# Two multiplications move from VectorE to GpSimd, one more pack of scores moves to VectorE, in a new order

## The chip, the core and the metric

The kernel runs on one core of one Trainium2 chip. The metric is the time of one execution on the device, in microseconds (us). The core's engines work side by side, each through its own queue in order: TensorE (PE in the profile, PEld for its weight loads), VectorE (DVE), ScalarE (ACT), GpSimd (POOL) and SyncE (SP, which issues the transfers). They wait for one another by semaphores. SBUF is the on-chip memory, PSUM the eight banks into which TensorE writes.

## What is computed

Two attention branches over the same x (2048 tokens, width 512, 32 heads of 16), mixed by a gate per token:

```python
def _A_ref(x, wqkv, wo):
    ...
    scores = jnp.einsum("bhqd,bhkd->bhqk", q, k) * (Dh ** -0.5)
    p = _softmax(scores, axis=-1)
    o = jnp.einsum("bhqk,bhkd->bhqd", p, v)
    ...
def _B_ref(x, wqkv, w_phi, wo):
    ...
    pq = jnp.einsum("bhsd,hdf->bhsf", q, w_phi)
    pk = jnp.einsum("bhsd,hdf->bhsf", k, w_phi)
    phi_q = jnp.concatenate([_softmax(pq, axis=-1), _softmax(-pq, axis=-1)], axis=-1)
    phi_k = jnp.concatenate([_softmax(pk, axis=-1), _softmax(-pk, axis=-1)], axis=-1)
    kv = jnp.einsum("bhsf,bhsd->bhfd", phi_k, v)
    z  = jnp.einsum("bhsf->bhf", phi_k)
    num = jnp.einsum("bhqf,bhfd->bhqd", phi_q, kv)
    den = jnp.einsum("bhqf,bhf->bhq", phi_q, z)[..., None] + 1e-6
    o = num / den
    ...
x = A_x
g = _sigmoid((x * gate_w).sum(-1, keepdims=True))
a = _A_ref(x, A_wqkv, A_wo)
b = _B_ref(x, B_wqkv, B_w_phi, B_wo)
return g * a + (1 - g) * b
```

Branch A is full attention: 32 heads x 2048 queries x 2048 keys of exponentials. Branch B is linear attention with "hedgehog" maps (the softmax of a projection and of its negative, over 16 features).

## The kernel before

**Packs and groups.** A unit is a tile of 128 keys by 512 queries of one head. A pack is four units: the same tile for four heads, whose matmuls run in four row or column quarters of TensorE. There are 512 packs: 4 chunks of queries, 8 sets of four heads, 16 tiles of keys; 32 groups `g` of 16 packs each (one chunk and one set of heads). Within a group the values are summed in one PSUM bank.

**Two ways to the exponential.** For most packs ScalarE computes it: `_qk` writes scores into a ring of five PSUM banks (`RING`), three and two units in turn, `_exp` (L1183) turns a group of them into ET in one instruction of 1536 or 1024 columns, `_pv` multiplies by the values. `self.mine` is the list of ScalarE's units; a unit's bank is its place in that list modulo 5. The scores of group k wait for the exponentials of group k - 2. The first five units and the last pack are done in two halves of 256 queries. `_last_pack` cuts the last four units in two pieces where the ring wraps inside them, and asks for all scores of a piece in one instruction, after the exponentials of the units that held its banks before (ScalarE's own lines there are L1070).

For the packs that `AWAY` names VectorE approximates: `_vector_bits` (L962, `v_bits`) converts each unit's scores to the bits of a power of two, and `_vector_terms` makes two more terms with shifted bits, by VectorE (L984, `v_term`, for a pair of packs in one instruction of 4096 elements, or 2048 for a single pack) and by GpSimd (L999, `p_term`, two instructions of 1024 per pack). Each such pack needs three rounds of value matmuls (L1250) where ScalarE's need one. `AWAY` has one number per group; each of its bits 0 to 4 names a tile of keys, and pack 510 is added at the end. Its 32 numbers have 130 bits set, in 76 pairs of which 22 are single.

**The end of a group.** `_norm` transposes the bank into T1 (L1271, `n_t1`), and for each two groups GpSimd multiplies the denominators with the gate (L1278, `n_den`), VectorE takes the reciprocal (L1280, `n_rec`) and multiplies the values with it into T2 (L1282, `n_mul`). Transfers turn T2 into onTA, which the output matmuls read (L651). Group 30 does this alone, group 31 in `_norm_last` in two halves (L1105 to L1117).

**Branch B.** `_b_quad` does four tiles of tokens at once: projections into bq (L1395), trees for maximum and minimum (L1414), subtraction (L1423), the exponentials on ScalarE (L1425), sums (L1430, L1432, and L1434 on GpSimd), and `_b_scale`, which gives reciprocals and multiplies half of bq with them: `b_rec`, `b_ratio` (on GpSimd), `b_mul` (L1450 for keys, L1455 for queries, VectorE, 2048 elements each). There are four quads for keys and four for queries. The maps then go to the key-value matmuls (L1473) or, by transposing transfers, to the numerator's (L1533).

**The order.** Nothing is ordered by hand in the instruction lists. Each operation is given to `Plan.op` with an engine, a cost in us, a due time in packs (`prio`) and an earliest time (`rel`), and `Plan.order` walks through time and picks for each engine what is ready and due first; the lists that it makes are the engines' programs. `SHIFT` moves the due times of named pieces (`b106`, `p102`, `x13`, ...) by up to 14 packs. Operations of GpSimd, and those of VectorE whose names are in `PORT` (`v_term`, `b_max`, `b_sub`, `b_sum`, `b_mul`, `n_mul` and others), are kept apart in the plan's time, and a GpSimd operation waits by semaphore for the last such operation of VectorE that the plan put ahead of it:

```python
if o.port:
    t = max(t, port, held.end + held.lat if held is not None and e == "POOL" else 0.0)
```

TensorE fills gaps with matmuls on zeros (L1257, `_fill`).

Of the kernel before, what the change touches and what calls it, by code (L numbers as in the profile page):

```python
# [7 lines left out]
ALU = mybir.AluOpType  # L8
AX = mybir.AxisListType

P = 128
# [378 lines left out]
class _Kernel:  # L390
# [364 lines left out]
    def _gate(self):  # L755
# [44 lines left out]
    AWAY = (26, 27, 26, 31, 22, 13, 15, 15, 31, 15, 13, 31, 30, 23, 31, 15, 29, 31, 26, 27, 31, 26, 31, 21, 31, 31, 28, 31, 31, 11, 23, 31)  # L800

    SHIFT = (
# [463 lines left out]
    def _norm(self, qc, src, side, last, dst, b_dst, due, job, alone=False):  # L1266

        op = self.plan.op
        T1, T2, rinv = self.T1, self.T2, self.rinv
# [6 lines left out]
        n, reads = hi - lo, b_T1[lo:hi]  # L1276
# [393 lines left out]
```

## Time and profile before

| | us |
|---|---|
| median of 3 runs | 737.42 (737.13 to 737.89) |
| profiled execution, whole | 737.4 |
| its span, first to last instruction | 735.6 |
| ScalarE busy | 723.5 |
| TensorE busy | 713.1 |
| VectorE busy | 690.5 |
| GpSimd busy | 303.8 |

The profile is one execution. A group's row has the line, the engine, the operation, what it writes and reads with its size, the count, the busy time in us, the mean of one in ns, and the idle time before it with what ended it. A timeline row has the start in us from the span's start, the length of a stretch of equal instructions and what they are; rows of one engine can overlap, since an instruction's record goes on while the next one starts. A wait's row names who waited for whom, the total in us, how many times, and the longest.

### The profile page before, as it was taken

How to read it: one execution, taken by the hardware profiler on the slowest of the kernel's cores; microseconds unless marked ns; L12 is line 12 of the kernel's file. 1: busy time of each engine (PE TensorE's matmuls, PEld its weight loads, DVE VectorE, ACT ScalarE, POOL GpSimd, SP SyncE). 2: the span in 40 equal slices, each digit the busy share in tenths (PEclk: the TensorE clock that was granted, in tenths of full speed). 3: DMA queues.
4: the chain of work that ended last, by engine and by line, in shares of the span. 5: the costliest groups of instructions: out<-in, count | busy, mean ns of one | idle time of the engine just before them, and what ended most of it. 6: DMA issues, size and time to landing. Idle time of an engine off the chain costs nothing.

```text
span 735.6 us, 19777 instructions
## 1 busy us (share of the span) xinstructions
PE 713.1 (97%) x8549; PEld 234.4 (32%) x8549; DVE 690.5 (94%) x1085; ACT 723.5 (98%) x636; POOL 303.8 (41%) x318
## 2 busy tenths in 40 slices
PE   8999999999999999999999999999999999999998
PEld 3334233243223223332232233333332233332322
DVE  4899999988999999999999999999999999999996
ACT  6999999999999999999999999999999999999996
POOL 3832342424544424535353344334334444344442
PEclk9999999999999999999999999999999999999999
DMA  9400100001010010100001032042123111003210
GB/s 201 145 10 6 22 2 9 16 4 18 4 15 11 4 20 2 17 11 8 14 2 17 15 61 28 8 83 35 23 45 74 21 16 23 16 25 63 40 29 30
DMA packets 90041, 21.96 MB, mean 30 GB/s; under 512 B 82913, under 2 KB 89441, under 8 KB 89953
## 3 DMA queue, kind: packets, MB, share of 16 engines
q1 hardware_dynamic: 88752, 20.30, 14.5%
q8 instruction: 67, 1.10, 0.7%
q10 hardware_dynamic: 1200, 0.39, 0.2%
q14 instruction: 22, 0.17, 0.1%
HBM read 4.21 MB, written 2.10 MB: 9 GB/s over the span
## 4 chain that ended last, share of the span: by engine, by line
ACT 73%; PE 13%; DVE 11%; DMA 1%; issue 0%; POOL 0%; DVEq 0%; POOLq 0%
ACT ET L1183 70%; PE ps L1131 5%; DVE va L962 4%; PE ps L1250 4%; ACT bq L1425 3%; PE ps L651 2%; DVE vp L984 2%; DVE btree L1414 1%; DMA xT<-in_A_x_dram 1%; PE ps L744 1%; PE ps L1257 1%; DVE bq L1423 0%; DVE VB L1541 0%; DVE nb L1541 0%; DVE rb L1539 0%
## 5 line engine op out<-in xcount | busy, mean ns | idle before, releaser
L1183 ACT ACTIVATE ET<-ps 128x1536 bf16<-128x1536 f32 (+1 forms) x612 | 692.9, 1343 | 4.6 <-PE ps L1131 4.4
L999 POOL TENSOR_SCALAR vp<-va 128x1024 uint16<-128x1024 uint16 x264 | 275.7, 1044 | 337.3 <-DVE vp L984 124.2
L962 DVE TENSOR_SCALAR va<-ps 128x512 uint16<-128x512 f32 x520 | 339.5, 681 | 23.9 <-PE ps L1131 21.7
L1131 PE MATMUL ps<-qT,kT 32*128 32x512 bf16 (+1 forms) x2053 | 311.0, 384 | 10.1 <-ACT ET L1183 5.1
L1131 PEld LDWEIGHTS ps<-qT,kT 32*128 32x128 bf16 x2053 | 82.7, 91 | 258.3 <-ACT ET L1183 146.5
L984 DVE TENSOR_SCALAR vp<-va 128x4096 uint16<-128x4096 uint16 (+1 forms) x151 | 162.0, 1079 | 0.6 <-PE ps L1250 0.2
L1250 PE MATMUL ps<-ET,V 128*32 128x512 bf16 x1532 | 149.0, 385 | 1.3 <-DVE T L1271 1.0
L1250 PE MATMUL ps<-vp,vc 128*32 128x512 bf16 x1040 | 93.9, 384 | 0.3 <-DVE vp L984 0.2
L1250 PEld LDWEIGHTS ps<-ET,V 128*32 128x32 bf16 x1532 | 39.3, 95 | 64.9 <-issue 48.6
L651 PE MATMUL ps<-WB,xT 128*32 128x512 bf16 x768 | 57.4, 382 | 0.5 <-DVE bq L1395 0.3
L1250 PE MATMUL ps<-va,V 128*32 128x512 bf16 x520 | 51.3, 385 | 0.0
L1250 PE MATMUL ps<-vp,V 128*32 128x512 bf16 x520 | 48.2, 383 | 0.3 <-DVE vp L984 0.2
L1257 PE MATMUL ps<-kT,zero 128*32 128x512 bf16 x468 | 42.1, 384 | 0.0
L651 PE MATMUL ps<-xT,WA 128*32 128x512 bf16 x480 | 36.1, 382 | 0.6 <-DVE va L962 0.4
L1250 PEld LDWEIGHTS ps<-vp,vc 128*32 128x32 bf16 x1040 | 24.7, 95 | 35.3 <-issue 20.2
L1425 ACT ACTIVATE bq<-bq 128x2048 bf16<-128x2048 bf16 x16 | 31.5, 1989 | 0.1
L1271 DVE STREAM_TRANSPOSE T<-ps 128x512 f32<-128x512 f32 x31 | 21.9, 708 | 1.1 <-PE ps L1250 1.0
L651 PE MATMUL ps<-WoB,WT 128*32 128x512 bf16 x256 | 22.6, 383 | 0.3 <-DVE va L962 0.3
L1395 DVE CAST bq<-ps 128x512 bf16<-128x512 f32 x32 | 21.7, 678 | 0.3 <-PE ps L651 0.2
L651 PEld LDWEIGHTS ps<-WB,xT 128*32 128x32 bf16 x768 | 15.2, 95 | 19.9 <-issue 10.4
L651 PE MATMUL ps<-WoA,onTA 128*32 128x512 bf16 x256 | 21.2, 381 | 0.0
L744 PE MATMUL ps<-WA,xT 128*128 128x128 bf16 x256 | 19.5, 220 | 0.7 <-DVE va L962 0.4
(94 smaller groups left out, 367.1 us busy)
## 6 DMA issues: line engine op xcount, KB each, us to landing
turned<-T SPq DMA_DIRECT2D x240, 8.0 KB, 1.8
qT<-qs SPq DMA_DIRECT2D x120, 16.0 KB, 1.8
WB<-in_B_wqkv_dram SPq DMA_DIRECT2D x1, 1536.0 KB, 6.9
out_dram<-WB SPq DMA_DIRECT2D x12, 128.0 KB, 2.0
WA<-in_A_wqkv_dram SPq DMA_DIRECT2D x3, 384.0 KB, 5.1
WoA<-in_A_wo_dram SPq DMA_DIRECT2D x1, 512.0 KB, 8.0
WoB<-in_B_wo_dram SPq DMA_DIRECT2D x1, 512.0 KB, 8.9
out_dram<-xT SPq DMA_DIRECT2D x3, 128.0 KB, 1.8
```

Source lines behind the costliest of these rows:

```text
L651: ins = e.matmul(out[32 * g:32 * g + 32], lhs[:, 32 * g:32 * g + 32], rhs, start=start, stop=stop, tile_position=(0, 32 * g), skip_group_c ...
L744: ins = e.matmul(self._bank(job)[:, P * tt:P * tt + P], self.xT[:, c, QCH * j + TOK * tt:QCH * j + TOK * tt + TOK], self.WA[:, 2, c, P * c ...
L962: parts.append(op("DVE", lambda e, j=j, job=job: e.tensor_scalar(self.va[:, pair, side, j, :], self._bank(job), SCALE * LOG2E * 128.0, (12 ...
L984: self.plan.op("DVE", lambda e, k=k, shift=shift: e.tensor_scalar(flat(self.vp[:, k]), flat(self.va[:, pair]), float(shift), None, op0=ALU ...
L999: o = self.plan.op("POOL", lambda e, flat=flat: e.tensor_scalar(flat[0], flat[1], 1.0, float(shift), op0=ALU.mult, op1=ALU.add), 0.08 + n ...
L1131: return e.matmul(out, self.kT[32 * i:32 * i + 32, cp, kt * TOK:(kt + 1) * TOK], self.qT[32 * i:32 * i + 32, s, at], start=True, stop=True ...
L1183: o = plan.op("ACT", lambda e: e.activation(self.ET[:, a % NS:a % NS + n, at], self.ps[:, self._ring(a):self._ring(a) + n, at], ACT.Exp, s ...
L1250: ins = e.matmul(self._bank(ot)[32 * i:32 * i + 32, at], V[:, v0:v0 + 32], tile(), start=(kt == 0), stop=(kt == self.NT - 1), tile_positio ...
L1257: ins = e.matmul(self._bank(ot)[32 * i:32 * i + 32, :], self.zero[:], self.kT[:, 0, 0:QCH], start=False, stop=False, tile_position=(0, 32 ...
L1271: self.turned_out = op("DVE", lambda e: e.transpose(T1[:, side].rearrange("p b s -> p (b s)"), src()), 0.635, deps=last, writes=[b_T1[side ...
L1395: [lambda e, b, k=k: e.tensor_copy(bq[:, k].rearrange("p (g s v) -> p g s v", g=8, s=2)[:, :, 0, :], b.rearrange("p (g v) -> p g v", g=8))],
L1425: op("ACT", lambda e, side=side: e.activation(sides[side], sides[side], ACT.Exp, scale=1.0 - 2 * side), self.c_act(2048) + 0.04, reads=[bu ...
```

## The change

1. `n_mul` is given to GpSimd, and its cost in the plan goes from 0.065 + 0.269 n to 0.31 + 0.3 n (n is 2 for a pair of groups, 1 for group 30).
2. `b_mul` is given to GpSimd, in two pieces of 1024 elements, each at a cost of 1.52.
3. `AWAY` has other numbers: 131 bits set, in 76 pairs of which 21 are single. `SHIFT` has other entries throughout.

```diff
-    AWAY = (26, 27, 26, 31, 22, 13, 15, 15, 31, 15, 13, 31, 30, 23, 31, 15, 29, 31, 26, 27, 31, 26, 31, 21, 31, 31, 28, 31, 31, 11, 23, 31)
+    AWAY = (22, 27, 13, 23, 11, 28, 26, 31, 31, 31, 14, 31, 31, 15, 29, 23, 15, 31, 22, 31, 27, 22, 31, 15, 30, 31, 30, 31, 30, 31, 11, 31)
...
-        op("DVE", lambda e: e.tensor_tensor(
+        op("POOL", lambda e: e.tensor_tensor(
             T2[:].rearrange("p b (s d) -> p s b d", s=2)[:, lo:hi], T1[:, lo:hi, :, 0:16],
-            rinv[:, lo:hi, :, None].to_broadcast([P, n, 16, 16]), ALU.mult), 0.065 + 0.269 * n,
+            rinv[:, lo:hi, :, None].to_broadcast([P, n, 16, 16]), ALU.mult), 0.31 + 0.3 * n,
            reads=reads + [b_rinv], writes=[b_T2], name="n_mul", prio=due)
...
         def run(name, cost, fn, at, reads, writes):
-            eng = "POOL" if name in ("b_ratio", "b_tot") else "DVE"
+            eng = "POOL" if name in ("b_ratio", "b_tot", "b_mul") else "DVE"
...
-                    ("b_mul", two(2048), lambda e: e.tensor_tensor(x[:, 0::2], x[:, 0::2], spread(r, 32), ALU.mult),
-                     b_r + both, [both[0]])]
+                    *[("b_mul", 1.52, lambda e, a=a: e.tensor_tensor(
+                        x[:, a:a + 32:2], x[:, a:a + 32:2], spread(r[:, a // 2:a // 2 + 16], 16), ALU.mult),
+                       b_r + both, [both[0]]) for a in (0, 32)]]
...
-                ("b_mul", two(2048), lambda e: e.tensor_tensor(x[:, 1::2], x[:, 1::2], spread(r, 32), ALU.mult),
-                 b_r + both, [both[1]])]
+                *[("b_mul", 1.52, lambda e, a=a: e.tensor_tensor(
+                    x[:, a + 1:a + 32:2], x[:, a + 1:a + 32:2], spread(r[:, a // 2:a // 2 + 16], 16), ALU.mult),
+                   b_r + both, [both[1]]) for a in (0, 32)]]
```

206 rows, old and new, of the table SHIFT are left out of this document.

## The prediction

> **What bounds the kernel now.** I read the page's busy times first, then the groups of ScalarE's instructions by shape, then what ScalarE waited for, then the chain that ended last.
>
> ```profile
> span 735.6 us, 19777 instructions
> PE 713.1 (97%) x8549; PEld 234.4 (32%) x8549; DVE 690.5 (94%) x1085; ACT 723.5 (98%) x636; POOL 303.8 (41%) x318
> ...
> ACT ET L1183 <- PE ps L1131: 4.4, 1, 4.4
> ACT xT L1619 <- PE ps L651: 2.9, 1, 2.9
> ...
> L1183 ACT ACTIVATE ET<-ps 128x1536 bf16<-128x1536 f32 x304 | 473.7, 1558 | 0.2
> L1183 ACT ACTIVATE ET<-ps 128x1024 bf16<-128x1024 f32 x303 | 344.8, 1138 | 0.0
> L1183 ACT ACTIVATE ET<-ps 128x512 bf16<-128x512 f32 x3 | 1.8, 601 | 0.0
> ...
> 550.71 94.97 ACT ET L1183 x84
> ...
> L1257 PE MATMUL ps<-kT,zero 128*32 128x512 bf16 x468 | 42.1, 384 | 0.0
> ```
>
> Three engines are over 90% busy, but only ScalarE (ACT) has no idle time between its start and its tail: it waits 4.4 us for the first scores and 2.9 us for the last output, and nowhere else by this view. PE's 97% holds filler work (468 matmuls of L1257), and VectorE has gaps. So a unit of exponentials (512 columns) taken from ScalarE shortens the run, if PE and VectorE go on feeding it. The records overlap at their ends, so the price of a group is the distance of two starts:
>
> ```profile
> 723.95 2.36 ACT L1183 ACTIVATE ET<-ps 128x1024 bf16<-128x1024 f32 x2
> 724.86 1.46 ACT L1183 ACTIVATE ET<-ps 128x1536 bf16<-128x1536 f32 x1
> ...
> 726.19 0.62 ACT L1183 ACTIVATE ET<-ps 128x512 bf16<-128x512 f32 x1
> 726.66 1.12 ACT L1070 ACTIVATE ET<-ps 128x256 bf16<-128x256 f32 x2
> 726.93 0.86 ACT L1070 ACTIVATE ET<-ps 128x768 bf16<-128x768 f32 x1
> ```
>
> A group of 1024 columns costs 0.91 us (723.95 to 724.86), one of 1536 1.33, one of 512 0.47: 2.24 for a pair of three and two units. The chain's stretch of 84 groups is 42 pairs of 2.26. The 0.02 between is small waiting that the records' overlap hides; over 303 pairs it is about 6 us, and it can shrink or grow.
>
> **The change part by part.** AWAY has 130 bits set before and 131 after: one more pack of four units goes to VectorE. ScalarE has 1528 units before: 5 in halves, 303 pairs of groups, then 3 + 1 left over, then the last pack's 4. After, 1524: 5, exactly 303 pairs, no leftover, and the last 4. The leftover groups go: 1.33 + 0.47 = 1.80 us less.
>
> The same arithmetic moves the end. Units sit in a ring of five banks. Before, the last pack starts in the fifth bank, so its scores go in two pieces, one unit and three, and the piece of three needs only banks that were freed one group earlier. After, it starts at unit 1520, bank 0, in one piece of four, and needs the banks of the last two groups, so it cannot start before the very last normal group is done.
>
> ```profile
> 7.09 0.28 PE L1131 MATMUL ps<-qT,kT 32*128 32x256 bf16 x3 [0.23 <-DVE qT L724]
> ...
> 7.42 9.61 ACT L1183 ACTIVATE ET<-ps 128x768 bf16<-128x768 f32 x10 [4.38 <-PE ps L1131]
> ...
> 726.37 0.39 PE L1131 MATMUL ps<-qT,kT 32*128 32x512 bf16 x3 [0.22 <-ACT ET L1183]
> ```
>
> PE starts 0.05 us after a group's record ends (724.86 + 1.46 = 726.32, then 726.37). From scores to exponential it is 0.33 us where nothing else holds it (7.09 to 7.42, 256 columns); full columns add 0.11 (0.39 against 0.28): 0.44. So the last group's start is followed not 0.91 but 1.14 + 0.05 + 0.44 = 1.63 us later by the last pack: 0.72 us of new idle time. The first half of the last pack then takes 1.14 as one group, as before (726.66 to 727.79). Net so far: -1.80 + 0.72 = -1.08 us.
>
> ```profile
> 726.92 1.04 POOL L999 TENSOR_SCALAR vp<-va 128x1024 uint16<-128x1024 uint16 x1 [1.85 <-DVE vp L984]
> ...
> 728.00 0.28 PE L1250 MATMUL ps<-ET,V 128*32 128x256 bf16 x4
> 728.02 0.10 PEld L1250 LDWEIGHTS ps<-vp,vc 128*32 128x32 bf16 x4
> ...
> 728.55 0.45 DVE L1105 STREAM_TRANSPOSE T<-ps 128x256 f32<-128x256 f32 x1 [1.72 <-PE ps L1250]
> ```
>
> The tail's first transpose also waits for the last term of pack 510, which GpSimd ends at 727.96: it starts at 728.55, while the values alone end at 728.28. Up to 0.27 us comes back if VectorE runs less late there; I take half, -0.15.
>
> VectorE loses eight b_mul and sixteen n_mul (g 0 to 29 in fifteen pairs, g 30 alone):
>
> ```profile
> L1282 DVE TENSOR_TENSOR T<-T,rinv 128x512 bf16<-128x512 f32 x15 | 10.4, 691 | 0.0
> L1455 DVE TENSOR_TENSOR bq<-bq,brec 128x2048 bf16<-128x2048 bf16 x4 | 4.8, 1212 | 0.0
> L1450 DVE TENSOR_TENSOR bq<-bq,brec 128x2048 bf16<-128x2048 bf16 x4 | 4.8, 1211 | 0.0
> ...
> 32.19 1.19 DVE va L962 x2
> ...
> L984 DVE TENSOR_SCALAR vp<-va 128x4096 uint16<-128x4096 uint16 x107 | 132.0, 1237 | 0.6 <-PE ps L1250 0.2
> L984 DVE TENSOR_SCALAR vp<-va 128x2048 uint16<-128x2048 uint16 x44 | 30.3, 695 | 0.1
> ```
>
> That is 20 us of records. It gains four bit conversions of 0.60 (two in 1.19) and, since one single pack becomes a pair, two additions that grow from 0.70 to 1.24: 3.5. VectorE falls by some 16 us, 2%. GpSimd gains them in other prices, which no row shows at these sizes:
>
> ```profile
> L999 POOL TENSOR_SCALAR vp<-va 128x1024 uint16<-128x1024 uint16 x264 | 275.7, 1044 | 337.3 <-DVE vp L984 124.2 <-DVE va L962 90.5 <-PE ps L1250 69.7
> L1434 POOL TENSOR_TENSOR bsum<-btree 128x256 f32<-128x256 f16 x8 | 4.9, 612 | 31.3 <-DVE vp L984 15.1 <-DVE btree L1432 11.1 <-DVE T L1282 5.0
> L1454 POOL TENSOR_TENSOR brec<-bsum 128x128 f16<-128x128 f32 x4 | 1.8, 456 | 1.8 <-DVE bsum L1453 1.6
> ...
> L1278 POOL TENSOR_TENSOR rinv<-T,gh x16: 258/264/1306, 64.8 to 712.9; 128x32 f32<-128x32 f32 x15, 128x16 f32<-128x16 f32 x1
> ...
>   PEld ps L1250: 2.2, 8
> ```
>
> Bounds for one b_mul piece of 1024 elements: 1.04 us (the one-input row of that size) and 2.45 (four times the two-input row of 256). From the two two-input rows the slope is 156 ns per 128 elements: 612 + 6 x 156 = 1.55 us, which I take, since they are the same kind of instruction; n_mul by the same slope 0.92, within 0.52 and 1.22. (From the 32-element row's median, 264, the slope is steeper: 1.55 ns per element, 1.80 us for a piece.) GpSimd gains 16 x 1.55 + 15.5 x 0.92 + two more terms of 1.04 = 41 us, to 345 of 734: never the bound by its sum.
>
> GpSimd's queue is in order: behind a multiply that waits for VectorE's reciprocal stand the terms of L999, for which PE's value matmuls wait. The last row is from the list of those who waited for L999: PE's weight loads, 2.2 us in all, so terms usually come early; the cover is that lead. The hedgehog maps come some 2 us later (two pieces of 1.55 for 1.21) to the transposes and to the key-value matmuls, which are due 2 steps of 3.45 packs, near 10 us, after the multiply. No cover, no such lead: each late term would stop PE for its delay. The extra pack costs PE two more rounds of four value matmuls, hidden in filler.
>
> The price that matters is what VectorE's two-input and 16-bit instructions and GpSimd's do to each other:
>
> ```profile
> 712.84 1.22 DVE L984 TENSOR_SCALAR vp<-va 128x4096 uint16<-128x4096 uint16 x1
> 712.89 1.25 POOL L1278 TENSOR_TENSOR rinv<-T,gh 128x16 f32<-128x16 f32 x1
> ...
> 720.96 1.04 POOL L999 TENSOR_SCALAR vp<-va 128x1024 uint16<-128x1024 uint16 x1 [1.16 <-DVE vp L984]
> ...
> 721.39 1.69 DVE L984 TENSOR_SCALAR vp<-va 128x4096 uint16<-128x4096 uint16 x1
> ```
>
> A product of 16 elements took 1.25 us because VectorE's addition was under way; an addition took 1.69 instead of 1.22 because GpSimd's term was. One holds the other off for its whole length. The order written out keeps them apart by its own costs (b_mul 1.52, n_mul 0.91), and the mean of 1237 against 1.22 shows that it mostly succeeds. With 1.55 and 0.92 it would still.
>
> [...]
>
> VectorE, freed of 16 us, holds PE up less. PE's own waits:
>
> ```profile
> PEld ps L1131 <- ACT ET L1183: 146.5, 365, 1.1
> ...
> PEld ps L1131 <- DVE va L962: 33.6, 98, 0.7
> ```
>
> Of ScalarE's 6 us of small waiting I let 0.5 go: an estimate, 2% less VectorE work and a new order that can as well be worse; bounds +1.5 and -3.
>
> Sum against the profiled execution's own 737.4 (span 735.6 and 1.8 around it; the median of the runs is 737.42): 737.4 - 1.08 - 0.15 - 0.5 = **735.7 us**.
>
> **The rivals.** (1) Slower: GpSimd's multiplies are longer than the order allows. At the upper bound of 2.45 us a piece holds the lock 0.93 us past its 1.52, and VectorE's next addition, tree step or subtraction stops for that; its conversions come late, PE stops in order behind their banks, ScalarE's next scores behind that. PE's lead over ScalarE is about 0.40 us (146.5 over 365 waits), so it decides from an overrun of 0.4 us, a piece of 1.9; n_mul's bound, 0.31 past its 0.91, stays below that. A hit costs 0.53; 16 of them 8.5 us, and with half falling where VectorE has conversions to do instead 4.2: 735.7 + 4.2 = 739.9. For it: the steeper slope, 1.80 a piece. Against: VectorE still has some 60 us idle to catch up in.
>
> (2) The relief gives nothing and the tail all of its idle time: -1.08 alone, or with 0.5 of worse waiting: 736.3 to 736.8. For it: 33.6 us of PE's waits are for conversions, of which there are more now.
>
> (3) The relief is worth more: half of the 6 us goes, as VectorE's gaps widen from 45 (735.6 - 690.5) to about 60 us: 737.4 - 1.08 - 0.27 - 2.7 = 733.4. Against: the conversions, the largest of PE's waits on VectorE, grow by four.
>
> (4) The leftover groups vanish but nothing else moves because the tail is bound by PE's output matmuls.
>
> ```profile
> 729.47 2.19 PE ps L651 x40
> ...
> 731.59 0.12 PEld L651 LDWEIGHTS ps<-WoA,onTA 128*32 128x32 bf16 x8 [0.46 <-DVE onTA L1117]
> ```
>
> Forty of them run without a break on the chain, with 0.46 us of spare time for weights before the last eight. An earlier VectorE would gain only that: 737.4 - 0.5 = 736.9.
>
> **How the numbers follow.** A measurement of this kernel can tell about 0.2% from no change: 735.9 to 738.9. The forecast has 0.40, own range 734.5 to 736.7, of which 0.28 lies below 735.9. (1) has 0.26, nearly all slower. (2) and (4) have 0.18 together, nearly all same. (3) has 0.16, all faster. That gives faster 0.46, same 0.29, slower 0.25. The range leaves out a tenth on each side: 733.2, just past (3), and 740.4, past the half-hit case of (1).
>
> **What would show it.** ET groups 303 and 303, none of 512; the last pack as two groups of 1024 after some 0.7 us of idle time (new in ScalarE's waits). L1450 and L1455 on GpSimd, 16 pieces near 1.55 us and n_mul near 0.92; the addition of 4096 still near 1237. VectorE's busy time near 674, GpSimd's near 345. A chain's pair at 2.26 or less. Pieces over 1.9 us, additions over 1.3 and pairs over 2.27 would make it wrong; so would a tail whose last pack follows at once.

## The result, and the profile after

| | before | after |
|---|---|---|
| median of the runs, us | 737.45 (737.05 to 738.39, 22 runs) | 738.51 (737.99 to 741.52, 22 runs) |
| profiled execution, us | 737.4 | 741.3 |
| its span, us | 735.6 | 739.3 |

The change makes the kernel slower by 0.2%: ratio 1.0020, 95% interval 1.0013 to 1.0028. The forecast was 735.7, faster. The time lies inside the range, but the direction is wrong. Four of the 22 executions after take 740.9 to 741.5 us, the other 18 take 738.0 to 739.3, and the profiled execution is one of the four. So two questions stand: what costs every run 2.8 us against the forecast, and what costs some of them 2.5 to 3 more.

The page's busy times, then ScalarE's and the moved operations' groups by shape, then what ScalarE waited for:

```profile
span 739.3 us, 19852 instructions
...
PE 716.6 (97%) x8581; PEld 234.5 (32%) x8581; DVE 683.8 (92%) x1065; ACT 722.8 (98%) x632; POOL 354.6 (48%) x352
```

```profile
L1181 ACT ACTIVATE ET<-ps 128x1536 bf16<-128x1536 f32 x303 | 471.7, 1557 | 3.2 <-PE ps L1129 2.9
L1181 ACT ACTIVATE ET<-ps 128x1024 bf16<-128x1024 f32 x303 | 344.5, 1137 | 0.6 <-PE ps L1129 0.5
...
L982 DVE TENSOR_SCALAR vp<-va 128x4096 uint16<-128x4096 uint16 x109 | 139.4, 1288 | 0.4 <-PE ps L1248 0.3
...
L982 DVE TENSOR_SCALAR vp<-va 128x2048 uint16<-128x2048 uint16 x42 | 30.6, 732 | 0.0
...
L1280 POOL TENSOR_TENSOR T<-T,rinv 128x512 bf16<-128x512 f32 x15 | 16.7, 1112 | 15.0 <-DVE rinv L1278 13.2 <-DVE vp L982 1.3
L1448 POOL TENSOR_TENSOR bq<-bq,brec 128x1024 bf16<-128x1024 bf16 x8 | 15.3, 1917 | 1.2 <-DVE vp L982 0.7
...
L1181 ACT ACTIVATE ET<-ps 128x512 bf16<-128x512 f32 x2 | 1.2, 592 | 0.0
```

```profile
ACT ET L1181 <- PE ps L1129: 8.5, 9, 5.1
...
ACT ET L1068 <- PE ps L1129: 0.6, 1, 0.6
```

(Lines are two lower than before, L1181 for L1183.) The work left ScalarE as the change says: 303 and 303 groups, one of 1536 fewer, and of 512 only the two halves at the start. But ScalarE now has idle time in the middle: 8.5 us of waits for scores in nine places, 5.1 of them at the start, where there was one wait of 4.4 at the start. The last row is the new idle time before the last pack. A piece of the hedgehog multiply takes 1.92 us, not 1.55, and the mean addition of 4096 elements 1288 ns, not 1237.

Two windows of 100 us, ScalarE's busy time alone, say where most of it is. First the kernel after, then the kernel before (window, its length, busy us and instructions, granted clock, share of the DMA engines, GB/s):

```profile
500.00:600.00 100.00, 97.83 (x86) 0.98 0.24 44
600.00:700.00 100.00, 99.42 (x88) 1.00 0.19 33
```

```profile
500.00:600.00 100.00, 99.91 (x88) 1.00 0.20 37
600.00:700.00 100.00, 99.98 (x89) 1.00 0.19 33
```

Of the two windows of after, the first has 2.2 us of idle time and a clock under 1.00, the second 0.6, which is one stop at 664 us. Another 0.7 of this execution lies at its very start (the longest wait, 5.1 against 4.4), where the first loads arrive; another kernel with this order, quoted below, has 4.27 there. An execution with this order's long pieces and the clock at 1.00 throughout (`sp_order` below) has 1.5 us of waits in the middle, in five places.

The stop at 664 us, at a query quad's pieces, in the timeline after:

```profile
657.29 1.92 POOL L1454 TENSOR_TENSOR bq<-bq,brec 128x1024 bf16<-128x1024 bf16 x1
...
659.17 1.06 POOL L1280 TENSOR_TENSOR T<-T,rinv 128x512 bf16<-128x512 f32 x1
...
660.31 2.17 POOL L997 TENSOR_SCALAR vp<-va 128x1024 uint16<-128x1024 uint16 x2
...
661.46 2.10 DVE L982 TENSOR_SCALAR vp<-va 128x4096 uint16<-128x4096 uint16 x1
...
663.61 0.10 PEld L1248 LDWEIGHTS ps<-vp,V 128*32 128x32 bf16 x4 [1.00 <-DVE vp L982]
...
664.38 3.71 ACT L1181 ACTIVATE ET<-ps 128x1536 bf16<-128x1536 f32 x3 [0.58 <-PE ps L1129]
```

GpSimd's queue runs without a gap from the second piece to 662.48: piece, `n_mul`, two terms. VectorE's addition starts at 661.46, one microsecond before the second term ends, and takes 2.10 us instead of 1.22. PE's value matmuls wait 1.00 us for it, and the next scores, behind them in PE's queue, leave ScalarE idle for 0.58 us. Here the piece itself held nobody off; the terms behind it came late and met the addition. At another stop, 85 us earlier, it is the piece that holds the addition off:

```profile
574.44 1.92 POOL L1454 TENSOR_TENSOR bq<-bq,brec 128x1024 bf16<-128x1024 bf16 x1
...
575.50 1.94 DVE L982 TENSOR_SCALAR vp<-va 128x4096 uint16<-128x4096 uint16 x1
```

PE waits 0.68 us for this addition, and ScalarE stops for 0.24 at 578.75. So there are two ways from the piece to the stop.

### The profile page after: what moved, and what is told of

The parts are those of the page before. It is cut to its first block, busy times and chain, and to the rows that moved or that the text cites. A ratio compares the mean times of both kernels' runs of the same rounds, so it can differ in the third digit from the quotient of the medians.

```text
span 739.3 us, 19852 instructions
## 1 busy us (share of the span) xinstructions
PE 716.6 (97%) x8581; PEld 234.5 (32%) x8581; DVE 683.8 (92%) x1065; ACT 722.8 (98%) x632; POOL 354.6 (48%) x352
## 4 chain that ended last, share of the span: by engine, by line
ACT 58%; PE 25%; DVE 15%; POOL 1%; issue 1%; DVEq 0%; POOLq 0%
ACT ET L1181 56%; PE ps L1129 8%; PE ps L1248 8%; DVE va L960 6%; PE ps L651 5%; DVE vp L982 4%; ACT bq L1423 2%; PE ps L1255 1%; PE ps L643 1%; DVE VB L1541 1%; DVE btree L1412 1%; POOL bq L1454 1%; DVE bq L1421 0%; PE ps L744 0%; POOL vp L997 0%
## 5 line engine op out<-in xcount | busy, mean ns | idle before, releaser
L1181 ACT ACTIVATE ET<-ps 128x1536 bf16<-128x1536 f32 (+1 forms) x610 | 693.6, 1343 | 8.9 <-PE ps L1129 8.5
L997 POOL TENSOR_SCALAR vp<-va 128x1024 uint16<-128x1024 uint16 x266 | 280.8, 1056 | 263.1 <-DVE vp L982 106.3
L982 DVE TENSOR_SCALAR vp<-va 128x4096 uint16<-128x4096 uint16 (+1 forms) x151 | 169.6, 1133 | 0.4 <-PE ps L1248 0.3
L1248 PE MATMUL ps<-vp,vc 128*32 128x512 bf16 x1048 | 95.6, 384 | 1.2 <-DVE vp L982 0.8
L1255 PE MATMUL ps<-kT,zero 128*32 128x512 bf16 x488 | 44.8, 387 | 0.0
L1423 ACT ACTIVATE bq<-bq 128x2048 bf16<-128x2048 bf16 x16 | 32.7, 2044 | 0.0
L1280 POOL TENSOR_TENSOR T<-T,rinv 128x512 bf16<-128x512 f32 (+1 forms) x16 | 17.3, 1082 | 15.1 <-DVE rinv L1278 13.2
L651 PE MATMUL ps<-WoB,WT 128*32 128x512 bf16 x256 | 20.9, 382 | 0.9 <-DVE WB L1622 0.7
```

The costliest lines, as they stand in the source:

```text
L651: ins = e.matmul(out[32 * g:32 * g + 32], lhs[:, 32 * g:32 * g + 32], rhs, start=start, stop=stop, tile_position=(0, 32 * g), skip_group_c ...
L982: self.plan.op("DVE", lambda e, k=k, shift=shift: e.tensor_scalar(flat(self.vp[:, k]), flat(self.va[:, pair]), float(shift), None, op0=ALU ...
L997: o = self.plan.op("POOL", lambda e, flat=flat: e.tensor_scalar(flat[0], flat[1], 1.0, float(shift), op0=ALU.mult, op1=ALU.add), 0.08 + n ...
L1181: o = plan.op("ACT", lambda e: e.activation(self.ET[:, a % NS:a % NS + n, at], self.ps[:, self._ring(a):self._ring(a) + n, at], ACT.Exp, s ...
L1248: ins = e.matmul(self._bank(ot)[32 * i:32 * i + 32, at], V[:, v0:v0 + 32], tile(), start=(kt == 0), stop=(kt == self.NT - 1), tile_positio ...
L1255: ins = e.matmul(self._bank(ot)[32 * i:32 * i + 32, :], self.zero[:], self.kT[:, 0, 0:QCH], start=False, stop=False, tile_position=(0, 32 ...
```

## The experiments

All are edits of the kernel after, each timed against the kernel before on the same chip. "Order" is the engines' programs as the plan wrote them; none of the edits below plans it anew, unless an instruction is inserted by hand. The line numbers of `sp_order` and `b_short_sp` are five higher than those of after.

**1. Pieces at the order's price (`b_short`).** Each piece multiplies 12 of its 16 rows; a quarter of the products is left out.

```diff
-                        x[:, a:a + 32:2], x[:, a:a + 32:2], spread(r[:, a // 2:a // 2 + 16], 16), ALU.mult),
+                        x[:, a:a + 24:2], x[:, a:a + 24:2], spread(r[:, a // 2:a // 2 + 12], 12), ALU.mult),
...
-                    x[:, a + 1:a + 32:2], x[:, a + 1:a + 32:2], spread(r[:, a // 2:a // 2 + 16], 16), ALU.mult),
+                    x[:, a + 1:a + 24:2], x[:, a + 1:a + 24:2], spread(r[:, a // 2:a // 2 + 12], 12), ALU.mult),
```

> The changed kernel with its order of instructions kept, but each b_mul piece multiplies 12 of its 16 rows (768 elements; a quarter of the products is left out). Theory A (the multiplications on GpSimd run longer than the order's costs, 1.92 us against 1.52 and 1.06 against 0.91; the overrun makes terms late, holds VectorE's additions off, and PE and ScalarE stop behind them): a piece takes about 1.49 us by the slope between the rows of 256 and 1024 elements, the order holds again around the pieces, and the time falls from 738.5 to about 737.2; VectorE's additions of 4096 elements fall from a mean of 1288 ns to about 1250. Theory B (the new order itself costs the time: transfers that stand late in SP's queue, and the last pack that cannot start before the group ahead of it is done): no change, 738.0 to 738.6.

Measured: 736.50 (735.88 to 738.62, 11 runs) beside 737.75; ratio 0.9988, interval 0.9979 to 0.9997. That is 2.0 us under the kernel after (2.3 if each is taken beside its own runs of the kernel before, 737.75 here and 737.45 there), and under the kernel before. The piece's group in its profile, then its timeline at the place shown above:

```profile
L1448 POOL TENSOR_TENSOR bq<-bq,brec 128x768 bf16<-128x768 bf16 x8 | 11.9, 1484 | 1.3 <-DVE vp L982 0.8
```

```profile
652.52 1.49 POOL L1454 TENSOR_TENSOR bq<-bq,brec 128x768 bf16<-128x768 bf16 x1
...
655.11 2.17 POOL L997 TENSOR_SCALAR vp<-va 128x1024 uint16<-128x1024 uint16 x2
...
657.10 1.25 DVE L982 TENSOR_SCALAR vp<-va 128x4096 uint16<-128x4096 uint16 x1
...
658.41 0.10 PEld L1248 LDWEIGHTS ps<-vp,V 128*32 128x32 bf16 x4 [0.56 <-DVE vp L982]
```

A piece of 1.48 fits the 1.52 that the order allows. Now the addition starts 0.18 us before the terms end (657.10 against 657.28), takes 1.25 us, and ScalarE has no idle time there. The chain that ended last changes with it, as the fourth part of the page shows for after and for this kernel:

```profile
ACT 58%; PE 25%; DVE 15%; POOL 1%; issue 1%; DVEq 0%; POOLq 0%
```

```profile
ACT 82%; PE 11%; DVE 6%; issue 0%; DVEq 0%
```

With the pieces at their price ScalarE carries the chain again; with the longer ones PE and VectorE have a quarter and a seventh of it. The fall of the clock in after's profiled execution is not the reason: `sp_order`, with the long pieces and the clock at 1.00, has ScalarE at 59% and PE at 25%.

The stops follow the additions. In after the additions that start at 432.77, 575.50 and 661.46 take 1.94 to 2.10 us, and a stop of ScalarE comes within 5 us of each; in `b_short` none of the three is over 1.3, and between the first scores and 709 us ScalarE has no idle time. Others stay long there and stop nothing (2.10 us at 428.91), so the mean of all 109 falls only to 1267 ns, not to the 1250 expected.

**2. Both multiplies at the order's price (`all_short`).** The same, and `n_mul` covers 13 of its 16 columns:

```diff
-            T2[:].rearrange("p b (s d) -> p s b d", s=2)[:, lo:hi], T1[:, lo:hi, :, 0:16],
-            rinv[:, lo:hi, :, None].to_broadcast([P, n, 16, 16]), ALU.mult), 0.31 + 0.3 * n,
+            T2[:].rearrange("p b (s d) -> p s b d", s=2)[:, lo:hi, :, 0:13], T1[:, lo:hi, :, 0:13],
+            rinv[:, lo:hi, :, None].to_broadcast([P, n, 16, 13]), ALU.mult), 0.31 + 0.3 * n,
...
```

The rest of T2 is set to zero once, at the start.

> As b_short, and n_mul multiplies 13 of 16 columns (416 elements; the rest of T2 stays zero). Theory A: n_mul takes about 0.89 us, all of GpSimd's multiplications are then at the order's costs, and the time is 736.2 to 737.0, below the kernel before. Theory B: 738.0 to 738.6, as without it.

Measured: 736.51 (735.69 to 738.18, 11 runs), ratio 0.9992 (0.9983 to 1.0001): the same as without it. `n_mul` goes from 1057 to 931 ns, and nothing follows from it. Its overrun of 0.15 us over the price of 0.91 costs nothing that these runs can tell.

**3. The last pack in two pieces again (`tail`).** Three units and one, as the ring had it before:

```diff
-        parts = [(cut, wrap), (wrap, cut + 4)] if cut < wrap < cut + 4 else [(cut, cut + 4)]
+        parts = [(cut, wrap), (wrap, cut + 4)] if cut < wrap < cut + 4 else [(cut, cut + 3), (cut + 3, cut + 4)]
```

> The changed kernel, whole, with the last pack in two pieces of three units and one, so that the piece of three needs only banks that were freed one group earlier. If the idle time ahead of the last pack sets the end: it goes (0.6 us of idle time in ScalarE's waits), the end comes 0.4 to 0.7 us earlier, about 738.0. If the tail is bound by the output matmuls and VectorE's last steps, or by the late terms of pack 510: the idle time goes, the time stays at 738.3 to 738.7.

Measured: 738.91 (738.04 to 741.68, 11 runs), ratio 1.0022 (1.0011 to 1.0033): no gain over the kernel after. The idle time does go. The timelines of the tail, first of after, then of this kernel:

```profile
730.95 1.94 ACT L1068 ACTIVATE ET<-ps 128x1024 bf16<-128x1024 f32 x2 [0.57 <-PE ps L1129]
...
732.14 0.28 PE L1248 MATMUL ps<-ET,V 128*32 128x256 bf16 x4
```

```profile
727.61 2.15 ACT L1068 ACTIVATE ET<-ps 128x768 bf16<-128x768 f32 x4
...
728.95 0.60 PE L1248 MATMUL ps<-vp,vc 128*32 128x512 bf16 x8
...
729.81 0.28 PE L1248 MATMUL ps<-ET,V 128*32 128x256 bf16 x4
```

The last pack's own value matmuls come 1.19 us after its first exponential in after (730.95 to 732.14) and 2.20 us here (727.61 to 729.81): PE is not done with the value rounds of the packs ahead, which stand before them in its queue. From the first of these exponentials to the end it is 8.35 us after (739.3 - 730.95) and 9.39 here (737.0 - 727.61). ScalarE starts the last pack without a pause, and PE uses up what that gave. The expectation had the output matmuls, VectorE's last steps or the late terms in this place.

**4. Transposes ahead of other transfers (`sp_order`).** After's SyncE queue and PE's wait behind it:

```profile
492.79 10.93 SPq L1288 DMA_DIRECT2D turned<-T  x16
503.76 1.32 SPq L1511 DMA_TRANSPOSE phiT<-bq  x1
...
508.36 2.68 SPq L1511 DMA_TRANSPOSE phiT<-bq  x2
```

```profile
514.59 0.32 PEld L1533 LDWEIGHTS ps<-kvbd,phiT 128*128 128x128 bf16 x8 [1.32 <-issue]
```

The four transposes of a query quad wait behind 16 transfers of another pair of groups; the last two are issued at 508.36 and 509.71, and PE stands idle until 514.6 ahead of the matmuls that read them. The row puts this wait down to nothing that it shows ("issue"), but the last transpose lands 4.8 us after its issue, at 514.5, where the other three took 3.1 to 3.3. In the profiled executions of `tail` and `b_short` the transposes stand as late, all four land after 3.1 to 3.3 us, PE reads them without this gap, and the clock stays at 1.00 there. In `tail` the last one is issued at 508.9 and read at 512.96: it has some 0.7 us to spare, and in after's execution it took 1.5 us longer than the others. The edit takes the transfers `dma_on321` and `dma_at321` (the values of one pair of groups) out of their place and puts them behind the quad's last transpose:

```diff
+            q = p.queues["SP"]
+            late = [o for o in q if o.name in ("dma_on321", "dma_at321")]
+            q[:] = [o for o in q if o not in late]
+            at = [o.name for o in q].index("dma_ph5") + 1
+            q[at:at] = late
```

> The changed kernel with one thing moved in SP's queue: the 16 transfers of T2 and the transpose behind them, which stand ahead of four transposes of the hedgehog maps near 495 us, are put behind those. Theory C (PE waits near 513.5 us for the last of these transposes; the gap of 1.05 us costs ScalarE time, and in about one run of five lets the granted clock fall, which makes those runs 741): the gap goes, no run is over 739.5, the granted clock is 1.00 throughout the profile, the median falls by 0.2 to 0.4 us. If the clock falls for another reason: still about one run of five near 741, and the median within 0.2 us of 738.5.

Measured: 738.50 (737.86 to 738.68, 11 runs), ratio 1.0009 (1.0000 to 1.0018). No run is above 738.68, where four of 22 were at 741. The median is after's 738.51, but beside a kernel before that took 737.75 and not 737.45 here; the expectation had 0.2 to 0.4 us of gain in it. The transposes now go first, in the queue of this kernel:

```profile
495.15 1.35 SPq L1516 DMA_TRANSPOSE phiT<-bq  x1
...
497.18 5.06 SPq L1516 DMA_TRANSPOSE phiT<-bq  x3
502.29 11.00 SPq L1293 DMA_DIRECT2D turned<-T  x16
```

So the runs at 741 come from the late transposes, and most of the loss in every run does not. (Of 40 executions of after, `tail` and `halves`, which have the late transposes, seven are over 740.8; of the 22 of this kernel and of number 6 none is more than 0.8 above its median. By chance alone all seven would fall among the 40 about once in 26 times.)

**5. The same time in shorter holds (`halves`).** Each piece becomes two instructions of 512 elements in the same place:

```diff
-                    *[("b_mul", 1.52, lambda e, a=a: e.tensor_tensor(
-                        x[:, a:a + 32:2], x[:, a:a + 32:2], spread(r[:, a // 2:a // 2 + 16], 16), ALU.mult),
+                    *[("b_mul", 1.52, [lambda e, a=a, h=h: e.tensor_tensor(
+                        x[:, a + h:a + h + 16:2], x[:, a + h:a + h + 16:2],
+                        spread(r[:, (a + h) // 2:(a + h) // 2 + 8], 8), ALU.mult) for h in (0, 16)],
...
```

> The changed kernel in its order; each b_mul piece of 1024 elements is issued as two instructions of 512, one right behind the other. If the price is the total time in GpSimd's queue (what stands behind comes late): two of 512 take about 2 x 1.06 = 2.12 us against 1.92, a further overrun of 0.2 for each of 16 pieces; by the slope that the shortened pieces showed (0.43 us less a piece gave 2.0 us) the time rises by about 0.9, to 739.4. If the price is the length for which one instruction holds VectorE off: VectorE's instructions get in between the halves, the hold is 1.06 instead of 1.92, and the time falls towards 737.

```profile
L1455 POOL TENSOR_TENSOR bq<-bq,brec 128x512 bf16<-128x512 bf16 x16 | 17.4, 1111 | 3.0 <-DVE vp L982 2.5
...
L1448 POOL TENSOR_TENSOR bq<-bq,brec 128x512 bf16<-128x512 bf16 x16 | 16.5, 1050 | 1.2 <-DVE vp L982 0.7
```

Measured: 739.36 (738.59 to 742.12, 7 runs), ratio 1.0027 (1.0016 to 1.0039). A single hold is now 1.05 to 1.11 us, shorter than even the 1.48 of `b_short`, but the two together take 2.1 to 2.2, and the kernel is not faster than after; it looks slower, though the intervals overlap. Where the piece itself held the addition, the halves help: VectorE's addition at 573.15 goes in between them, takes 1.22 us, and the stop near 578 is gone. Elsewhere the stops stay. So on the whole it counts more how late GpSimd's queue goes on than how long one instruction holds VectorE off.

**6. Both losses away (`b_short_sp`).** The edits of 1 and 4 together.

> Both edits at once: each GpSimd piece of the hedgehog maps multiplies only 12 of its 16 rows (768 elements, 1.48 us; a quarter of the maps' halves stays without its reciprocal), and the two transfers of groups 30 to 31 (onTA) stand behind the transposes of the next quad in SyncE's queue. Theory A (two separate losses: pieces over their price, 2.0 us in the median, and late transposes, which cost time in some runs alone): median 736.0 to 736.5, no run over 737.5, clock 0.999 to 1.000 in every run. Rival (the runs of the short pieces at 738 have another cause, or moving the transfers makes those transfers' readers late): median unchanged at 736.5 and still runs near 738 at clock 0.997, or a median over 736.8.

Measured: 735.99 (735.65 to 736.76, 11 runs) beside 737.70; ratio 0.9978 (0.9969 to 0.9987). The few runs of `b_short` near 738 are gone with the late transposes, and the median is 0.5 lower: the two losses add up. Whether the late transposes cost anything in the other runs stays open. Beside their own runs of the kernel before, the medians of 4 and 6 are 0.3 and 0.5 better than those of after and of 1, but the intervals overlap. Its page's first line, and ScalarE's first and last wait for scores in its timeline:

```profile
span 733.7 us, 19853 instructions
```

```profile
7.32 13.08 ACT L1186 ACTIVATE ET<-ps 128x768 bf16<-128x768 f32 x13 [4.27 <-PE ps L1134]
```

```profile
725.34 1.94 ACT L1073 ACTIVATE ET<-ps 128x1024 bf16<-128x1024 f32 x2 [0.58 <-PE ps L1134]
```

**7. The multiplies, or a part of them, back on VectorE.** If the pieces are too long for GpSimd, VectorE could take the rest without a new plan. Six kernels try it. In `quarter` GpSimd does 12 of 16 rows as in `b_short`, and VectorE does the other four rows of each half, two instructions of 256 elements per quad, put into its list ahead of the next instruction that is kept apart from GpSimd's; `quarter2` puts them ahead of the next instruction of any kind. `b_back` and `b_back2` give VectorE the whole multiply in these two ways. `quarter_sp` and `quarter2_sp` add the edit of 4.

```diff
+            fn = [lambda e, x=x, r=r, a=a, odd=odd: e.tensor_tensor(
+                x[:, a + odd:a + 8:2], x[:, a + odd:a + 8:2],
+                r[:, a // 2:a // 2 + 4, None, :].to_broadcast([P, 4, DH, 4]), ALU.mult) for a in (24, 56)]
...
+            at = next(i for i, d in enumerate(dve) if d.port and d.start >= o.start)
+            dve.insert(at, o)
```

> The changed kernel in its order, whole: GpSimd multiplies 12 of the 16 rows of each b_mul piece (about 1.48 us, at the order's cost of 1.52), VectorE the remaining 8 rows of a quad (two instructions of 256 elements, about 0.5 us), ahead of the first two-input or 16-bit instruction after the second piece. If the overrun is the cause: as with the shortened pieces, plus little for VectorE's 4 us: 736.4 to 737.2, faster than the kernel before. If the new instructions push VectorE late: 737.5 or more.

> The changed kernel in its order, with b_mul back on VectorE as one instruction of 2048 elements per quad (1.21 us), put ahead of the first two-input or 16-bit instruction that stands in VectorE's list from the time of the first piece on. n_mul stays on GpSimd, and the 131 packs stay. If b_mul on GpSimd is the cause of the loss: GpSimd's queue is 31 us lighter, VectorE's 10 us heavier, and the time is 736.3 to 737.3. If VectorE's relief was what carried the 131st pack: 738 or more.

> As quarter, with the transfers moved in SP's queue as in sp_order. If the wait for the late transposes still costs: 0.2 to 0.5 us below quarter and a narrower spread of the runs. If it costs nothing when the pieces fit: equal to quarter within 0.2 us.

> As quarter, but VectorE's two instructions of a quad stand ahead of its very next instruction after the second piece, not of the next two-input or 16-bit one. In quarter the trace has one stop of ScalarE of 4.5 us and one of 1.2 near 440 us, where the first query quad's maps came 5 us later than the transposes and PE stood in order behind them. If that misplacement was the loss, and the overrun is the cause of the changed kernel's: both stops go, and the time is 736.4 to 737.4, at or below the kernel before. If any instruction added to VectorE's list costs what the shorter pieces gave: 738 to 739.

> As quarter2, with the transfers moved in SP's queue as in sp_order: within 0.3 us of quarter2, without runs that stand 2.5 us above the others.

> As b_back (b_mul whole on VectorE, 1.21 us per quad, n_mul on GpSimd, 131 packs, the order kept), but the instruction stands ahead of VectorE's very next instruction from the time of the first piece on, so that the maps are not later than with GpSimd. If b_mul on GpSimd was the loss: 736.4 to 737.5. If the order needs VectorE's relief: 738.5 or more, with conversions late behind each of the eight.

| | median, us | ratio to before |
|---|---|---|
| `quarter` | 743.53 (4 runs) | 1.0082 (1.0069 to 1.0095) |
| `quarter_sp` | 742.63 | 1.0067 (1.0054 to 1.0080) |
| `quarter2` | 742.83 (739.53 to 744.42, 7 runs) | 1.0056 (1.0036 to 1.0077) |
| `quarter2_sp` | 744.35 | 1.0092 (1.0079 to 1.0105) |
| `b_back` | 748.60 (746.72 to 752.82, 5 runs) | 1.0160 (1.0137 to 1.0182) |
| `b_back2` | 746.73 (742.87 to 750.88) | 1.0125 (1.0094 to 1.0156) |

Every one is slower than the kernel after. The expectations that a part of the work on VectorE would come out near `b_short` were wrong by 5 us and more; and moving the transfers changed the time by -0.9 and +1.5 us, where 0.2 to 0.5 of gain or no change, and a difference within 0.3, were expected. The groups of `quarter` and `b_back` give the inserted work (L440), and the timeline of `quarter` its largest stop (L1200 is after's L1181, L1532 its L1511, L1554 its L1533):

```profile
L440 DVE TENSOR_TENSOR bq<-bq,brec 128x256 bf16<-128x256 bf16 x16 | 5.5, 386 | 0.0
```

```profile
L440 DVE TENSOR_TENSOR bq<-bq,brec 128x2048 bf16<-128x2048 bf16 x8 | 11.0, 1380 | 0.0
```

```profile
429.52 1.35 DVE L440 TENSOR_TENSOR bq<-bq,brec 128x256 bf16<-128x256 bf16 x2
430.90 5.36 SPq L1532 DMA_TRANSPOSE phiT<-bq  x4
...
438.20 0.24 PEld L1554 LDWEIGHTS ps<-kvbd,phiT 128*128 128x128 bf16 x4 [4.19 <-DMA phiT<-bq]
...
440.16 1.02 ACT L1200 ACTIVATE ET<-ps 128x1024 bf16<-128x1024 f32 x1 [4.36 <-PE ps L1148]
```

The transposes can go only after VectorE's part, at 430.90, and PE, in order, waits 4.19 us for them. That is a misplaced instruction, and it explains `quarter` alone: in `quarter2`, where the part stands ahead of VectorE's next instruction, this stop is gone and the median hardly better. Beside the 736.50 of `b_short`, 5.5 us of work put into VectorE's list cost 7.0 us (`quarter`) and 11.0 us cost 12.1 (`b_back`), though VectorE is idle for 55 us in all (739.3 - 683.8).

A part of this is not the work but TensorE's clock. Over the whole execution its mean is 0.981 to 0.998 in all runs of the six kernels but three, where `b_short` has 0.997 to 1.000. The three are runs of `quarter2` at 1.000: they take 739.5 to 740.0 us, the other four, at 0.992 to 0.995, 742.8 to 744.4. In one of those four (length; PE, PEld, DVE, ACT, POOL busy; clock; DMA share; GB/s):

```profile
502.00:504.00 2.00, 2.00 (x18) 0.52 (x19) 0.73 (x2) 1.49 (x2) 1.35 (x2) 0.50 0.16 20
```

PE is busy throughout at half its clock, and ScalarE, which needs its scores, is idle for a quarter of the time. So `quarter2` without the clock's fall costs 3.0 to 3.5 us beside `b_short`. For the other five kernels the two parts were not told apart, and how each of the other stops arises was not followed further.

## Why the prediction was wrong

**The price of a piece is the step that failed.** The prediction took 1.55 us for 1024 elements, from the slope between the rows of 128 and 256 elements (456 and 612 ns, 156 per 128). The rows that the runs add are 1057 ns for 512 (`n_mul`, in `b_short`), 1484 for 768 and 1917 for 1024: 433 ns per 256 elements, or 1.69 per element, against 1.22 from the two rows taken. The row of 128 elements is the product of a reciprocal with other types, so its difference to the row of 256 was no slope of one kind of instruction. The steeper slope that the prediction named as an aside (1.80 a piece) was nearer, and the upper bound of 2.45 too high.

**The first rival is what happened, at its threshold.** It was to decide from an overrun of 0.4 us, a piece of 1.9; the overrun is 0.40 and the piece 1.92. Taking it away brings 2.0 to 2.3 us. The rival's own price was 4.2, for an overrun of 0.93. Its mechanism, the lock by which one engine's instruction holds the other's off, is there whole at 575 us: the piece holds VectorE's addition off (1.94 us, where the median of the 109 is 1.22), PE waits in order (0.68), ScalarE's scores stand behind (0.24). But it is only half of what happens: at 657 to 664 the piece holds nothing and pushes GpSimd's queue back, and the terms behind it collide with the addition; `halves`, which takes the first kind away at that place and makes GpSimd's queue later still, gains nothing. That VectorE has gaps to catch up in was no protection, since the stop is where PE needs that one addition. The test "additions over 1.3" was too coarse: the mean rose only to 1288, and a mean over 109 hides a few of some 2 us. A two-input instruction of VectorE is held too: in the kernel before, the subtraction of 2048 elements (L1423) that starts at 270.80, while a term of GpSimd is under way until 271.34, takes 1.61 us, where the median of the 16 is 1.21.

**`n_mul` at 0.92** was 1.06, and this costs nothing that `all_short` can tell, as the prediction had it for an overrun below 0.4.

**The groups, -1.80,** went as forecast: 303 and 303.

**The end, +0.72 and -0.15.** The idle time is there, 0.57 to 0.62 for 0.72. But it is not a loss. From the first exponential of the last pack to the end it was 8.94 us before (735.6 - 726.66) and is 8.36 in `b_short_sp` (733.7 - 725.34): 0.58 comes back, not 0.15. `tail` shows why: the end hangs on PE's value rounds, which use the pause. The fourth rival had the right engine, but named the output matmuls; and it cost the change nothing that the groups gave.

**The relief, -0.5,** did not come. In `b_short_sp` the time from the first exponential to the end is 726.38 us (733.7 - 7.32), before it was 728.18 (735.6 - 7.42). The difference of -1.80 is what the groups alone were to give, with the end at zero (+0.58 - 0.58). VectorE's busy time fell to 683.8 and not to 674: the additions alone are 170.0 us where they were 162.3.

**The sum, then, was right by luck** for the kernel that it described: with the pieces at 1.5 us and the transposes in time the medians differ by -1.71 (737.70 to 735.99), and the forecast was -1.7, but its loss at the end (+0.72 - 0.15) and its relief (-0.5), neither of which came, cancel. The order's price was the fault, and the prediction accepted it because its own reading of the rows agreed.

**The late transposes** were not among the steps: SyncE's queue was not followed, and the new order puts 16 transfers ahead of a quad's transposes in SyncE's queue. They add 2.5 to 3 us to about one run in five; what they cost the other runs, if anything, is 0.3 to 0.5 by the medians and stays open.

A version with the whole multiplies that beats the kernel before was not found. Not tried: an order searched with the true price of 1.92 in the plan.

## What to carry to other kernels

Price a moved operation at its own size and from rows of its own kind; where two slopes can be drawn, work the change out with the steeper one as well, and see whether the sign holds. In an order written out by costs, an overrun of a few tenths counts where the queue behind is full (here 0.40 us a piece, for 2.0 to 2.3 us in the medians): look at what stands behind the longer instruction in its in-order queue and with whom that will collide, more than at the instruction itself. Work put by hand into such an order can cost a large part of its length or more, by stops and by a lower clock, however much that engine idles elsewhere (here 5.5 us of it cost 7.0 and 11.0 cost 12.1, at mean clocks of 0.993 to 0.995 and 0.987 to 0.998 where `b_short` has 0.997 to 1.000), so a remainder handed to another engine needs a new plan.

## What the runs showed of the hardware

TensorE's granted clock fell to 0.50 in the middle of dense work. The windows of after around the wait for the transposes (length; PE, PEld, DVE, ACT, POOL busy; clock; DMA share; GB/s):

```profile
512.00:514.00 2.00, 1.27 (x9) 0.28 (x5) 2.00 (x5) 2.00 (x3) 1.04 (x1) 1.00 0.30 62
514.00:516.00 2.00, 1.38 (x19) 0.68 (x23) 2.00 (x5) 1.45 (x2) 0.26 (x1) 0.88 0.10 25
516.00:518.00 2.00, 2.00 (x23) 0.32 (x15) 0.38 (x2) 1.07 (x2) 1.05 (x1) 0.50 0.28 59
518.00:520.00 2.00, 1.77 (x23) 0.34 (x16) 0.93 (x2) 1.90 (x2) 0.30 (x1) 0.77 0.20 31
```

PE was busy for 2.65 of 4 us, with one gap of 1.05 to 1.3 us, and then ran at half clock for more than 2 us: (0.12 + 0.50 + 0.23) x 2 = 1.7 us of its work lost, more than the gap itself. In the third window the clock is 0.50. With the transposes ahead (`sp_order`), where PE is busy for 3.70 us from 512 to 516, and in the execution of `tail` where they landed in time, PE has no such gap and the clock stays at 1.00 in these windows. How little PE must do for the clock to fall, no run here measures.

GpSimd's two-input multiply with a broadcast second input grows by 1.69 ns per element in the pieces (1484 ns for 768 elements of bf16 in `b_short`, 1917 for 1024 in after, in place) and by 1.70 in `n_mul` (621 ns for 256 elements in after, 1057 for 512 in `b_short`, one input of f32): a fixed part of some 0.19 us (1917 - 1024 x 1.69).
